# Deferring the second LayerNorm of the later half of the tokens into the first down projection

## Chip, cores, metric

One core of one Trainium2 chip for each run; the experiments ran in three groups, each on its own chip with its own runs of the kernel before. The metric is the device time of one execution in microseconds (us), median of several runs. The engines are called PE (matrix multiply), DVE (vector), ACT (scalar activation), Pool (GpSimd) and SP (whose queue issues all DMAs of this kernel).

## The reference

A linear attention block and a gated MLP, each behind a LayerNorm, with residuals; S = 2048 tokens, D = 1024, F = 3584, bf16.

```python
h  = x + attention(layernorm(x)) @ wo            # 32 heads, phi(t) = elu-like feature map
n  = layernorm(h)
h2 = h + (relu(n @ W_gate) * (n @ W_up)) @ W_down
```

## The kernel before

The tokens are 16 tiles of 128. The attention half of the kernel walks over tile steps `t`. At step `t` PE computes the numerators of tile `t` (`a2`, eight short matmuls), DVE divides (`dtmp`, `rden`, three products), a DMA transposes the result, and two steps later (`LAG = 2`) PE applies the output projection (`a4`, 16 matmuls of 512 columns) and DVE adds the residual. In steps 0 to 10 two query projections (`a1`, 8 matmuls each, with an exp on ACT and two DVE operations behind them) fill PE. Then the MLP runs in two passes of 1024 tokens: first 14 gate/up pairs by a Strassen scheme that needs sums of activations (S sums) and of weights (T sums), then four down rounds of 24 us.

```python
        def a4(st):
            ...                                  # 16 matmuls into a pair of banks
            PL.add("dve", ... name="h_%d" % st)  # hsb = psum + x2  (residual)
            dma(sl_hs[hs], h_scr[st * P:(st + 1) * P, :], hsb[:, hs, :], "st_h_%d" % st, ...)
            ks = ln_stats(hsb[:, hs, :], ...)    # DVE: 2 bn_stats, aggregate, +eps; Pool: rstd (pow)
            PL.add("pool", ... name="nmr_%d" % st)          # -mean * rstd
            ...
        def a4_norm(st):                         # one step later
            PL.add("act", ... name="norm2_%d" % st)         # ACT: xn = rstd * h + nmr
            if st < TPP:                         # first 8 tiles: straight to the MLP's input
                dma_t(sl_tx[kx], hnT[:, :, st * P:(st + 1) * P], xn[:, kx, :], "T5d_%d" % st, ...)
            else:                                # later 8 tiles: scratch copy for the second pass
                dma(sl_tx[kx], hn_scr[(st - TPP) * P:(st - TPP + 1) * P, :], xn[:, kx, :], ...)
        ...                                      # (cut)
        for t in range(NST + LAG + 1):
            if t >= LAG + 1:
                a4_norm(t - LAG - 1)
            if t < NST:
                a2(t)
            if rest:
                a1(*rest.pop(0))
            if LAG <= t < NST + LAG:
                a4(t - LAG)
            if rest:
                a1(*rest.pop(0))
            if t == 13:
                s_sums()                         # DVE, 4 x 1.2 us
            if t == 15:
                for f_ in t_sums(0) + t_sums(1): # DVE, 8 x 0.42 us
                    f_()
        ...                                      # (cut) d_round: seven steps of 16 matmuls
            for c in range(NFB):
                ...                              # 16 matmuls; in the last step also the evictions
                load_wd_next()                   # next weight tile, 4 steps ahead
                if fill:
                    fill.pop(0)()                # extra work handed in, one piece a step
```

In the traces the instructions of an engine start in the order in which the program lists them.

## Time and profile before

| | |
|---|---|
| median time | 801.71 us (801.42 to 802.7, 3 runs) |
| PE busy | 777.7 of the profiled 800.3 us (97%) |
| DVE / ACT / Pool busy | 54% / 31% / 3% |
| chain that ended last | 91% PE, 5% DVE |

PE is full nearly everywhere; the exception is the seam between attention and MLP. The table of windows of the kernel before shows it (columns: window and length, then busy us and instruction count of PE, PE weight loads, DVE, ACT and Pool, then the granted PE clock, DMA share and GB/s):

```profile
core 0: us, PE busy (x) PEld busy (x) DVE busy (x) ACT busy (x) POOL busy (x), PEclk, DMA share, GB/s
200.00:225.00 25.00, 24.66 (x135) 11.93 (x134) 23.05 (x52) 8.20 (x10) 3.07 (x8) 1.00 0.56 142
225.00:250.00 25.00, 17.35 (x83) 7.55 (x84) 23.23 (x47) 3.72 (x3) 4.65 (x8) 0.87 0.68 157
250.00:275.00 25.00, 20.08 (x84) 8.57 (x84) 17.24 (x37) 9.88 (x13) 2.74 (x7) 0.93 0.53 179
```

PE loses 7.6 us in the second and 4.9 us in the third window, and the clock is below 1.00 there, while DVE is nearly full in the first two. The PE timeline of the kernel before shows where (columns: start, length, engine, line, operation, count; in brackets the idle time before it and what ended it):

```profile
start us, us, engine line op out<-in xcount [idle before <-releaser]
...
220.22 0.63 PE L499 MATMUL ps<-kvz,RAB 128*128 128x132 bf16 x8
...
235.99 3.61 PE L499 MATMUL ps<-RW,RO 128*128 128x512 bf16 x15
245.15 1.45 PE L499 MATMUL ps<-kvz,RAB 128*128 128x132 bf16 x8 [5.55 <-DVE RO L674]
246.39 12.43 PE L499 MATMUL ps<-RW,RO 128*128 128x512 bf16 x47
258.66 1.89 PE L499 MATMUL ps<-hnT,wring 128*128 128x512 bf16 x8
260.39 1.89 PE L499 MATMUL ps<-RC,RE 128*128 128x512 f16 x8
267.10 3.42 PE L499 MATMUL ps<-RC,RE 128*128 128x512 f16 x8 [4.82 <-ACT ps L762]
270.31 1.89 PE L499 MATMUL ps<-hnT,wring 128*128 128x512 bf16 x7
```

At warm pace 16 matmuls of 512 columns take 3.45 us to the start of the next group. So 5.55 us are lost before 245.15, 4.82 us before 267.10, and matmuls after each of these gaps are slow (eight took 3.21 us to the next group's start instead of 1.73). The first gap has its cause in DVE, as the DVE timeline of the kernel before shows: the S sums (L735) stand ahead of the division (L663) of the tile that PE wants next:

```profile
238.87 2.36 DVE L735 TENSOR_TENSOR RC<-hnT 128x2048 f16<-128x2048 bf16 x2
241.26 1.22 DVE L735 TENSOR_TENSOR RC<-RC,hnT 128x2048 f16<-128x2048 f16 x1
242.52 1.23 DVE L735 TENSOR_TENSOR RC<-hnT,RC 128x2048 f16<-128x2048 bf16 x1
243.67 0.38 DVE L663 TENSOR_SCALAR dtmp<-ps 128x24 f32<-128x24 f32 x2
```

The second gap is a chain: residual, statistics of the last tile, rstd, norm2 on ACT, and only then ACT's first copy for the MLP, which PE waits for. Its end, in the ACT timeline of the kernel before (L717 is norm2, L762 the copies):

```profile
265.32 1.24 ACT L717 ACTIVATE xn<-hsb,nmr,rstd 128x1024 bf16<-128x1024 bf16 x1 [1.91 <-POOL nmr L706]
266.46 1.06 ACT L762 ACTIVATE ps<-ps 128x512 f32<-128x512 f32 x2
```

As one yardstick for the seam, take the time from `a2` of tile 11 (220.22) to the MLP's second product on the plain weights (270.31): 50.09 us. At warm pace it is 5 x 0.47 (`a2`) + 7 x 3.45 (`a4`) + 3 x 1.73 (the first three MLP products) = 31.7 us. The seam loses 18.4 us, 2.3% of the kernel.

### The profile page before, as it was taken

The numbers are of one execution on the slowest core, as the hardware profiler recorded it, in microseconds if no ns is written. First come the engines' busy times: TensorE is split into PE (matmuls) and PEld (weight loads), VectorE is DVE, ScalarE is ACT, GpSimd is POOL, SyncE is SP. The second block draws the span as 40 slices with busy tenths as digits, with TensorE's granted clock in tenths as the row PEclk, the third lists the DMA queues.
The fourth block names the chain that finished last, engine by engine and source line by source line (L and its number), as shares of the span: only waits on it lengthen the run. The fifth ranks groups of instructions, "written<-read, shape, count | busy, mean of one in ns | idle before, by whom it ended". The sixth has DMA issues, their size and how long they took to land.

```text
span 800.3 us, 9969 instructions
## 1 busy us (share of the span) xinstructions
PE 777.7 (97%) x3719; PEld 360.3 (45%) x3791; DVE 432.3 (54%) x900; ACT 246.8 (31%) x402; POOL 25.2 (3%) x60
## 2 busy tenths in 40 slices
PE   8999999999987799999999999999999999999998
PEld 3444444444433344444444444444444444444443
DVE  7455535799999656756755103137657657401111
ACT  4333333232321455455453000024454454400000
POOL 2000000010111000000000000000000000000000
PEclk9999999999998999999999999999999999999999
DMA  9777300155574523223234896643133132035662
GB/s 302 197 182 199 94 14 1 34 139 140 140 174 127 188 74 105 77 83 106 69 89 131 230 243 211 206 135 106 54 105 104 55 106 80 0 125 192 209 207 82
DMA packets 160128, 102.37 MB, mean 128 GB/s; under 512 B 50384, under 2 KB 153040, under 8 KB 160080
## 3 DMA queue, kind: packets, MB, share of 16 engines
q1 hardware_dynamic: 160080, 101.73, 43.9%
q8 instruction: 30, 0.49, 0.3%
q14 instruction: 18, 0.15, 0.1%
HBM read 79.69 MB, written 10.49 MB: 113 GB/s over the span
## 4 chain that ended last, share of the span: by engine, by line
PE 91%; DVE 5%; issue 1%; DMA 1%; ACT 1%; SPq 0%; POOL 0%; DVEq 0%; POOLq 0%; ACTq 0%
PE ps L499 91%; DVE st L509 1%; DVE hsb L698 1%; DVE RO L674 1%; DMA RAB<-in_A_wqkv_dram 1%; ACT RX L533 1%; DVE RAB L538 1%; DVE RC L735 0%; DVE RX L535 0%; DVE RE L751 0%; DVE rden L667 0%; DVE dtmp L663 0%; SPq L432 0%; DVE mv L512 0%; PE ps L568 0%
## 5 line engine op out<-in xcount | busy, mean ns | idle before, releaser
L499 PE MATMUL ps<-RW,RAB 128*128 128x512 bf16 x878 | 192.8, 379 | 0.9
L499 PE MATMUL ps<-RC,RE 128*128 128x512 f16 x672 | 155.9, 382 | 4.8 <-ACT ps L762 4.8
L499 PEld LDWEIGHTS ps<-RW,RAB 128*128 128x128 bf16 x896 | 87.7, 98 | 105.7
L499 PE MATMUL ps<-RAB 128*128 128x512 bf16 x499 | 112.4, 379 | 1.7 <-ACT RAB L571 0.7
L762 ACT ACTIVATE ps<-ps 128x512 f32<-128x512 f32 x112 | 65.1, 582 | 152.9 <-PE ps L499 149.1
L868 DVE TENSOR_TENSOR RX<-ps,RX 128x512 bf16<-128x512 f32 x32 | 22.0, 691 | 166.1 <-PE ps L499 145.3
L499 PE MATMUL ps<-hnT,wring 128*128 128x512 bf16 x448 | 106.0, 379 | 0.0
L499 PEld LDWEIGHTS ps<-RC,RE 128*128 128x128 f16 x672 | 66.0, 98 | 85.2 <-ACT ps L762 5.3
L762 ACT ACTIVATE RO<-ps 128x512 f32<-128x512 f32 x112 | 66.7, 597 | 53.7 <-PE ps L499 53.7
L812 DVE TENSOR_TENSOR RAB<-ps,RAB 128x512 bf16<-128x512 f32 x28 | 19.4, 691 | 112.8 <-PE ps L499 112.8
L499 PEld LDWEIGHTS ps<-RAB 128*128 128x128 bf16 x512 | 49.2, 98 | 58.0 <-ACT RAB L571 0.9
L499 PEld LDWEIGHTS ps<-hnT,wring 128*128 128x128 bf16 x448 | 43.9, 98 | 53.3 <-issue 0.8
L533 ACT ACTIVATE RX<-ps 128x512 bf16<-128x512 f32 x64 | 38.0, 594 | 92.5 <-PE ps L499 65.8
L499 PE MATMUL ps<-RW,RO 128*128 128x512 bf16 x249 | 59.1, 388 | 0.4
L499 PE MATMUL ps<-RAB,RC 128*128 128x512 bf16 x250 | 58.0, 379 | 0.3
L499 PE MATMUL ps<-RC,wring 128*128 128x512 f16 x224 | 52.9, 379 | 0.0
L762 ACT ACTIVATE RAB<-ps 128x512 bf16<-128x512 f32 x56 | 33.4, 597 | 62.2 <-PE ps L499 62.2
L535 DVE TENSOR_SCALAR RX<-RX 128x512 bf16<-128x512 bf16 x64 | 18.4, 288 | 58.6 <-ACT RX L533 58.6
L499 PE MATMUL ps<-hnT,RE 128*128 128x512 bf16 x196 | 46.9, 379 | 1.5
L751 DVE TENSOR_TENSOR RE<-wring,RE 128x512 f16<-128x512 bf16 x112 | 47.0, 420 | 1.9
L751 DVE TENSOR_TENSOR RE<-wring 128x512 f16<-128x512 bf16 x112 | 42.0, 416 | 0.0
L819 DVE TENSOR_TENSOR RO<-ps,RO 128x512 f32<-128x512 f32 x56 | 38.7, 691 | 5.5 <-ACT RO L762 5.4
(56 smaller groups left out, 486.3 us busy)
## 6 DMA issues: line engine op xcount, KB each, us to landing
RW<-in_B_W_down_dram SPq DMA_DIRECT2D x56, 512.0 KB, 3.7
wring<-in_B_W_gate_dram SPq DMA_DIRECT2D x28, 512.0 KB, 3.7
wring<-in_B_W_up_dram SPq DMA_DIRECT2D x28, 512.0 KB, 4.7
RAB<-in_A_wqkv_dram SPq DMA_DIRECT2D x8, 512.0 KB, 8.4
RX<-in_A_x_dram SPq DMA_DIRECT2D x16, 256.0 KB, 3.1
h_scr<-hsb SPq DMA_DIRECT2D x16, 256.0 KB, 3.3
RX<-h_scr SPq DMA_DIRECT2D x32, 128.0 KB, 3.7
out_dram<-RX SPq DMA_DIRECT2D x32, 128.0 KB, 1.7
```

Source lines behind the costliest of these rows:

```text
L499: lambda e: e.matmul(out_ap, lhsT, rhs, start=start, stop=stop, skip_group_check=skip),
L509: PL.add("dve", lambda e, c=c: e.bn_stats(out=st6[:, k, c * 6:(c + 1) * 6], in_=src_full[:, c * BCH:(c + 1) * BCH]), reads=[src_chunk_bufs ...
L533: PL.add("act", lambda e: e.activation(out=Et[:, k, 0:w], in_=src, func=ACTF.Exp), reads=[B_bank[b]], writes=[B_E[k]], name=name + "_exp")
L535: PL.add("dve", lambda e: e.tensor_scalar(out=E2t[:, k, 0:w], in0=Et[:, k, 0:w], scalar1=1.0, scalar2=1e-6, op0=ALU.min, op1=ALU.add), rea ...
L538: PL.add("dve", lambda e: e.scalar_tensor_tensor(out=dst_ap, in0=src, scalar=C1, in1=E2t[:, k, 0:w], op0=ALU.add, op1=ALU.max), reads=[B_b ...
L674: lambda e, nbk=nbk, g0=g0, ng=ng: e.tensor_tensor(out=osb[:, k, g0 * P:(g0 + ng) * P].rearrange("p (g h e) -> p g h e", g=ng, e=Dh), in0= ...
L698: PL.add("dve", lambda e: e.tensor_tensor(out=hsb[:, hs, :], in0=ps[:, b:b + 2, :], in1=x2[:, xs, :].rearrange("p (a c) -> p a c", a=2), o ...
L751: PL.add("dve", lambda e: e.tensor_tensor(out=Tring[:, k, j], in0=in0, in1=in1, op=ALU.subtract), reads=reads, writes=[B_T[k][j]], name="T ...
L762: PL.add("act", lambda e: e.activation(out=dst, in_=src, func=func), reads=reads, writes=writes, name=name)
L812: PL.add("dve", lambda e: e.tensor_tensor(out=hh[:, f1, 0:SBW], in0=bank(BA[1]), in1=r11[:, rr, :], op=ALU.mult), reads=[B_bank[BA[1]], B_ ...
L819: PL.add("dve", lambda e, w=w: e.tensor_tensor(out=ftmp[:, 4 + w, :], in0=bank(BF_[w]), in1=ftmp[:, 2 + w, :], op=ALU.add), reads=[B_bank[ ...
L868: PL.add("dve", lambda e: e.tensor_tensor(out=outst[:, k, :], in0=bank(banks4[j], NW), in1=hres[:, k, :], op=ALU.add), reads=[B_bank[banks ...
```

## The change

The LayerNorm of tiles 8 to 15 is needed only in the second MLP pass. The change takes it out of the seam, where DVE is short, and puts it into the first two down rounds, where DVE is nearly idle (before the change 2.77 us busy in 450 to 475): each of ten down steps loads one tile of `h` back, computes statistics on the tile before it, and normalizes (on DVE) and transposes the tile before that. The scratch copy of the normalized tiles goes away. The first eight T sums go to Pool at step 8, and the S sums come one step earlier.

```diff
+            if st >= TPP:
+                return                          # in a4: no statistics for tiles 8..15
             ks = ln_stats(hsb[:, hs, :], [B_hs[hs]] * NBC, "ln2_%d" % st)
...
-            else:
-                dma(sl_tx[kx], hn_scr[...], xn[:, kx, :], "st_hn_%d" % st, ...)
+        def late_ln(i):
+            def load(t):
+                dma(sl_hl[t % 2], hl[:, t % 2, :], h_scr[(TPP + t) * P:(TPP + t + 1) * P, :], ...)
+            def stats(t):
+                late_k[t] = ln_stats(hl[:, t % 2, :], [B_hl[t % 2]] * NBC, ...)
+            def norm(t):
+                ln_norm_dve(late_k[t], hl[:, k, :], [B_hl[k]], xl[:, k, :], B_xl[k], ...)
+                dma_t(sl_xl[k], hnT[:, :, t * P:(t + 1) * P], xl[:, k, :], "T5d_%d" % (TPP + t), ...)
+            if 0 <= i - 2 < TPP:
+                norm(i - 2)
+            if i < TPP:
+                load(i)
+            if 0 <= i - 1 < TPP:
+                stats(i - 1)
...
-            if t == 13:
+            if t == 8:
+                for f_ in t_sums(0, "pool") + t_sums(1, "pool"):
+                    f_()
+            if t == 12:
                 s_sums()
-            if t == 15:
-                for f_ in t_sums(0) + t_sums(1):
-                    f_()
...
-                    for t in range(i * STB, (i + 1) * STB):
-                        late.append(... dma_t(..., hn_scr[t * P:(t + 1) * P, :], "T5s_%d" % t, ...))
+                    for t in range(i * NFB, (i + 1) * NFB):
+                        late.append(lambda t=t: late_ln(t))
```

(`hl` and `xl` lie in memory that the attention half no longer uses.)

More of the change, by code (lines that the diff above doesn't have):

```diff
@@ L191, in bass_sequential_preLN__linear_attn_block__glu_gated_reglu__prompt_kernel @@
     h_scr = nc.dram_tensor("h_scr", [S, D], bf16).ap()
-    hn_scr = nc.dram_tensor("hn_scr", [S // 2, D], bf16).ap()
     es = ExitStack()
@@ L243, in bass_sequential_preLN__linear_attn_block__glu_gated_reglu__prompt_kernel @@
         Tring = RE[:, 0:NTR * 4 * KH * P].bitcast(f16).rearrange("p (s j k c) -> p s j k c", s=NTR, j=4, k=KH)
+        o0 = NTR * 4 * KH * P
+        hl = RE[:, o0:o0 + 2 * D].rearrange("p (a b) -> p a b", a=2)
+        xl = RE[:, o0 + 2 * D:o0 + 4 * D].rearrange("p (a b) -> p a b", a=2)
         RO = sb("RO", [P, 2 * NO * D], bf16)
@@ L305, in bass_sequential_preLN__linear_attn_block__glu_gated_reglu__prompt_kernel @@
         sl_hs = slots("dhs_", NHS)
-        sl_ht = slots("dht_", TPP)
+        sl_hl = slots("dhl_", 2)
+        sl_xl = slots("dxl_", 2)
         def bufs(name, n):
@@ L331, in bass_sequential_preLN__linear_attn_block__glu_gated_reglu__prompt_kernel @@
         B_hscr = bufs("hscr_", NST)
-        B_hnscr = bufs("hnscr_", TPP)
+        B_hl = bufs("hl_", 2)
+        B_xl = bufs("xl_", 2)
         B_st6 = [bufs("st6_%d_" % k, NBC) for k in range(NSTAT)]
@@ L362, in flat @@
             return [b for row in x for b in (flat(row) if isinstance(row, list) else [row])]
-        for b_ in flat(B_T):
+        for b_ in flat(B_T) + B_hl + B_xl:
             b_.over = flat(B_x1) + flat(B_pk) + flat(B_v)
@@ L421, in bass_sequential_preLN__linear_attn_block__glu_gated_reglu__prompt_kernel @@
         PL.add("pool", lambda e: e.memset(vv[:, :, :, P:VW], 1.0), writes=[B_vones], name="vones")
-        for b_ in flat(B_T):
+        for b_ in flat(B_T) + B_hl + B_xl:
             b_.over = b_.over + [B_vones]
@@ L719, in a4_norm @@
                    reads=[B_hs[hs], B_nmr[ks], B_rstd[ks]], writes=[B_xn[kx]], name="norm2_%d" % st)
-            if st < TPP:
-                dma_t(sl_tx[kx], hnT[:, :, st * P:(st + 1) * P], xn[:, kx, :], "T5d_%d" % st, reads=[B_xn[kx]],
-                      writes=[B_hnT[st]])
-            else:
-                dma(sl_tx[kx], hn_scr[(st - TPP) * P:(st - TPP + 1) * P, :], xn[:, kx, :], "st_hn_%d" % st,
-                    reads=[B_xn[kx]], writes=[B_hnscr[st - TPP]])
+            dma_t(sl_tx[kx], hnT[:, :, st * P:(st + 1) * P], xn[:, kx, :], "T5d_%d" % st, reads=[B_xn[kx]],
+                  writes=[B_hnT[st]])
+        late_k = {}
+        def late_ln(i):
+            def load(t):
+                dma(sl_hl[t % 2], hl[:, t % 2, :], h_scr[(TPP + t) * P:(TPP + t + 1) * P, :], "ld_hl_%d" % t,
+                    reads=[B_hscr[TPP + t]], writes=[B_hl[t % 2]])
+            def stats(t):
+                late_k[t] = ln_stats(hl[:, t % 2, :], [B_hl[t % 2]] * NBC, "ln2_%d" % (TPP + t))
+            def norm(t):
+                k = t % 2
+                ln_norm_dve(late_k[t], hl[:, k, :], [B_hl[k]], xl[:, k, :], B_xl[k], "ln2_%d" % (TPP + t))
+                dma_t(sl_xl[k], hnT[:, :, t * P:(t + 1) * P], xl[:, k, :], "T5d_%d" % (TPP + t), reads=[B_xl[k]],
+                      writes=[B_hnT[t]])
+            if 0 <= i - 2 < TPP:
[4 more added lines that the diff above has]
+                stats(i - 1)
         def s_sums():
@@ L741, in s_sums, with t_sums @@
             add(3, blk(1, 0), Ssum[:, 1], ALU.subtract, [B_S[1]] + bl(0))
-        def t_sums(L):
+        def t_sums(L, eng="dve"):
             i = L % NWG
@@ L750, in add @@
             def add(j, in0, in1, reads):
-                PL.add("dve", lambda e: e.tensor_tensor(out=Tring[:, k, j], in0=in0, in1=in1, op=ALU.subtract),
+                PL.add(eng, lambda e: e.tensor_tensor(out=Tring[:, k, j], in0=in0, in1=in1, op=ALU.subtract),
                        reads=reads, writes=[B_T[k][j]], name="T%d_%d" % (j + 1, L))
@@ L964, in bass_sequential_preLN__linear_attn_block__glu_gated_reglu__prompt_kernel @@
         for t in range(NST + LAG + 1):
-            if t >= LAG + 1:
+            if LAG + 1 <= t < TPP + LAG + 1:
                 a4_norm(t - LAG - 1)
@@ L994, in bass_sequential_preLN__linear_attn_block__glu_gated_reglu__prompt_kernel @@
                 if p_ + 1 < NPASS and i < 2:
-                    for t in range(i * STB, (i + 1) * STB):
-                        late.append(lambda t=t: dma_t(
-                            sl_ht[t], hnT[:, :, t * P:(t + 1) * P], hn_scr[t * P:(t + 1) * P, :],
-                            "T5s_%d" % t, reads=[B_hnscr[t]], writes=[B_hnT[t]]))
+                    for t in range(i * NFB, (i + 1) * NFB):
+                        late.append(lambda t=t: late_ln(t))
                 if p_ + 1 < NPASS and i == 2:
```

## The prediction

> **What bounds the kernel now.** TensorE. The page has PE busy for 777.7 of 800.3 us (97%), and the chain that ended last is 91% PE. It is full (24.9 of every 25 us, clock 1.00) everywhere except in the first microseconds and at the seam between attention and MLP: the table of 25 us windows shows 17.35 us busy at 225-250 (clock 0.87) and 20.08 at 250-275 (clock 0.93). There DVE is busy for 23.2 and 17.2 us. The PE timeline at the seam shows idle stretches of 0.8 us at three tiles, 5.55 us at 239.6 (DVE does the four S sums, 4.9 us, ahead of a tile's division) and 4.82 us at 262.3 (PE waits for ACT's first copy, which stands behind norm2 of the last tile, hence behind that tile's statistics). About 5 us more go to matmuls that run slower after the gaps (47 in 12.4 us; warm pace 16 in 3.45). Against an ideal pace the seam loses some 17-18 us. That is all this change can win.
>
> **Removed.** For 8 tiles: two bn_stats of 0.69, aggregate 0.21, add 0.15 = 1.7 us of DVE each, 14 us in all; rstd 0.55 + nmr 0.27 on Pool; norm2 1.24 on ACT; one 256 KB store. Eight T sums (0.42 us each, 3.4 us) leave DVE. Once the a1 projections run out (tile step 11 on) a step needs 5.3 us of DVE against 4.05 us of PE; without LayerNorm DVE needs 3.7, so PE becomes the limit. The 4.82 us wait at the end disappears.
>
> **Kept.** The S sums still sit before a tile's division, one step earlier: about 4-5 us of PE wait, 1-2 us of it again in slow matmuls.
>
> **New cost 1, Pool.** Eight tensor_tensor of 512 elements per partition. No such Pool op is in this trace. The Trainium skill, "GPSIMD Engine Reference", section 3.1, gives 4497 ns for 2048 elements; my estimate from it is 1.1-1.3 us each, 9-11 us together, starting at about 208 us. rstd of tile 7 queues behind them (218-219 us instead of 214.6), norm2 of tile 7 on ACT is late, the exp behind it too, then DVE, then the bank pair for the next output projection: I charge 2-3 us of PE wait near 221. The skill's "SBUF — State Buffer" (section Who interferes with whom) says that DVE and Pool lock a shared port pair; the trace agrees so far: rstd took 1.60 us instead of 0.55 beside the S sums. A few e2 ops (0.29 us) on DVE may wait about 1 us each.
>
> **New cost 2, the first down rounds.** 8 x (1.7 + 0.54 norm) = 18 us of DVE where DVE is nearly idle (2.8 of 25 us), 2 MB more reads. DMA is already at 0.9-1.2 there while transposes run, but weight tiles are issued four steps (about 10 us) ahead; I expect PE to stay full: 0-1 us.
>
> **Sum.** 17.5 - 5.5 (S sums with slow clock) - 2.5 (Pool) + about 1.5 (other) = about 11 us saved: 790.7 us, range 786.5 to 795.5. Faster by over 2%: 0.09; within 2%: 0.89; slower: 0.02.
>
> **What would show it.** The first MLP matmul at about 247-250 us instead of 258.7, with no wait for ACT after it; one remaining gap of 3.5-5 us around 232-236, released by DVE; Pool T sums above 1 us each and a PE gap of 2-3 us near 221; PE full from 425 to 535 us.
>
> **What would make it wrong.** Pool sums at 2 us or more each (S sums then wait for tile 7's transpose, several us back); or at 0.6 us (2-3 us more gain); DMA saturation in the first down rounds starving the weights; the clock staying low after the gap.

## The result

| | before | changed |
|---|---|---|
| median time | 802.08 us (801.42 to 802.7, 4 runs) | 792.8 us (792.4 to 793.36, 4 runs) |
| ratio | 1 | 0.9885 (95%: 0.9868 to 0.9902) |
| profiled span | 800.3 us | 790.9 us |
| seam (50.09 us before) | loses 18.4 us | loses 7.7 us |

A ratio is the mean time of one kernel's runs over that of the other's of the same rounds, so it is not quite the ratio of the medians. The change is 1.15% faster: clear of the noise, and within 2%.

The windows of the changed kernel (the last line is in the down rounds):

```profile
core 0: us, PE busy (x) PEld busy (x) DVE busy (x) ACT busy (x) POOL busy (x), PEclk, DMA share, GB/s
...
225.00:250.00 25.00, 20.79 (x108) 9.54 (x109) 20.26 (x36) 0.00 (x0) 0.00 (x0) 0.93 0.68 155
250.00:275.00 25.00, 25.00 (x117) 11.35 (x116) 13.74 (x27) 10.44 (x18) 0.00 (x0) 1.00 0.50 158
...
450.00:475.00 25.00, 23.85 (x112) 10.51 (x110) 12.73 (x26) 0.00 (x0) 2.19 (x4) 1.00 0.94 252
```

DVE is no longer full at the seam and PE gained 3.4 and 4.9 us there; the third window is full. A small new loss stands at 450-475. The PE timeline of the changed kernel at the seam:

```profile
220.29 0.63 PE L504 MATMUL ps<-kvz,RAB 128*128 128x132 bf16 x8
...
225.08 0.35 PE L504 MATMUL ps<-kvz,RAB 128*128 128x132 bf16 x3 [0.71 <-DVE RO L679]
...
226.26 3.62 PE L504 MATMUL ps<-RW,RO 128*128 128x512 bf16 x16
...
230.79 3.63 PE L504 MATMUL ps<-RW,RO 128*128 128x512 bf16 x16 [0.45 <-DMA RO<-RO]
237.38 0.35 PE L504 MATMUL ps<-kvz,RAB 128*128 128x132 bf16 x3 [2.96 <-DVE RO L679]
...
238.56 5.30 PE L504 MATMUL ps<-RW,RO 128*128 128x512 bf16 x16
243.70 0.63 PE L504 MATMUL ps<-kvz,RAB 128*128 128x132 bf16 x8
...
254.53 1.89 PE L504 MATMUL ps<-hnT,wring 128*128 128x512 bf16 x8
...
259.71 1.89 PE L504 MATMUL ps<-hnT,wring 128*128 128x512 bf16 x8
```

From 220.29 to 259.71 are 39.42 us, 7.7 us over the 31.7 us of warm pace. Three things make it up:

- From the end of the projection before it (about 224.2 at warm pace) to 226.26, 2.04 us pass for an `a2` of 0.47 us: 1.57 us lost. At 230.79 another 0.6 us, where a transpose came late.
- At 234.24 (230.79 + 3.45) PE stops until 237.38 for the division of tile 13, behind the S sums; `a4` starts at 238.56 instead of 234.71: 3.85 us.
- The 16 matmuls after it take 243.70 - 238.56 = 5.14 us instead of 3.45: 1.69 us of low clock.

The sum is 7.71 us. The wait for ACT before the MLP is gone. The Pool timeline of the changed kernel shows the first item's origin, the sums (L777, two in a line) between rstd of tile 6 and rstd of tile 7 (L522):

```profile
207.27 0.55 POOL L522 TENSOR_TENSOR rstd<-ve,neghalf 128x1 f32<-128x1 f32 x1 [6.46 <-DVE ve L519]
...
208.50 2.27 POOL L777 TENSOR_TENSOR RE<-wring 128x512 f16<-128x512 bf16 x2 [0.32 <-issue]
...
215.33 2.43 POOL L777 TENSOR_TENSOR RE<-wring,RE 128x512 f16<-128x512 bf16 x2
217.72 0.55 POOL L522 TENSOR_TENSOR rstd<-ve,neghalf 128x1 f32<-128x1 f32 x1
```

One Pool sum took 1.13 to 1.22 us, and rstd of tile 7, at 214.57 before, came at 217.72.

The loss in the down rounds is one gap of PE, 1.15 us, and what ended it was a weight load:

```profile
423.74 38.15 PE L504 MATMUL ps<-RW,RAB 128*128 128x512 bf16 x176
463.04 58.94 PE L504 MATMUL ps<-RW,RAB 128*128 128x512 bf16 x272 [1.15 <-DMA RW<-in_B_W_down_dram]
```

The DMA issues of the changed kernel around it (RW is the weight ring; columns as in the timeline, length is the issue's time in the queue):

```profile
447.84 1.48 SPq L441 DMA_TRANSPOSE hnT<-RE  x1
...
450.81 2.12 SPq L437 DMA_DIRECT2D out_dram<-RX  x4
453.03 0.39 SPq L437 DMA_DIRECT2D RW<-in_B_W_down_dram  x1
...
455.43 1.92 SPq L437 DMA_DIRECT2D RX<-h_scr  x4
457.44 0.38 SPq L437 DMA_DIRECT2D RW<-in_B_W_down_dram  x1
```

A step of the round takes 3.45 us, so with the round beginning at 423.74 PE ends its seventh step at about 447.9 and its eighth at 451.3 (estimates by that count; in the first step the load went out 0.3 us after the time so counted, at 427.45). The weight loads that these ends allow were issued at 453.03 and 457.44, 5 and 6 us late; the second landed 5.55 us after its issue, by the chain of waits, at 462.99, and PE went on at 463.04. What stood ahead of it in the queue: a transpose of a deferred tile (1.2 to 1.5 us of queue time each; its own wait is for norm on DVE), four output stores that waited for evictions (on DVE these began at 450.09, behind the statistics of a deferred tile, which had waited for its load until 448.45), and four residual loads (1.92 us).

The two ends meet: the seam gained 18.4 - 7.7 = 10.7 us, the down rounds lost 1.2 us, so 9.5 us should be gained; the spans differ by 9.4 us.

### The profile page after: what moved, and what is told of

The parts are those of the page before. It is cut to its first block, busy times and chain, and to the rows that moved or that the text cites. A ratio compares the mean times of both kernels' runs of the same rounds, so it can differ in the third digit from the quotient of the medians.

```text
span 790.9 us, 10017 instructions
## 1 busy us (share of the span) xinstructions
PE 779.6 (99%) x3791; PEld 360.0 (46%) x3791; DVE 434.4 (55%) x900; ACT 237.3 (30%) x394; POOL 30.5 (4%) x60
## 4 chain that ended last, share of the span: by engine, by line
PE 95%; DVE 2%; issue 1%; DMA 1%; SPq 1%; ACT 0%; POOL 0%; DVEq 0%; POOLq 0%
PE ps L504 95%; DMA RW<-in_B_W_down_dram 1%; DVE RO L679 1%; DVE RC L761 0%; SPq L437 0%; DVE RX L894 0%; PE ps L573 0%; DVE hsb L703 0%; SPq L441 0%; DVE rden L672 0%; DVE dtmp L668 0%; DVE RX L540 0%; ACT RX L538 0%; DVE RAB L543 0%; POOL hsb L399 0%
## 5 line engine op out<-in xcount | busy, mean ns | idle before, releaser
L504 PE MATMUL ps<-RC,RE 128*128 128x512 f16 x672 | 154.2, 380 | 0.0
L540 DVE TENSOR_SCALAR RX<-RX 128x512 bf16<-128x512 bf16 x64 | 19.5, 305 | 61.3 <-ACT RX L538 61.2
L504 PE MATMUL ps<-hnT,RE 128*128 128x512 bf16 x224 | 52.9, 380 | 0.0
L777 DVE TENSOR_TENSOR RE<-wring,RE 128x512 f16<-128x512 bf16 x108 | 45.5, 421 | 1.8
L777 DVE TENSOR_TENSOR RE<-wring 128x512 f16<-128x512 bf16 x108 | 40.6, 418 | 0.0
```

What stands on the lines that cost most here:

```text
L504: lambda e: e.matmul(out_ap, lhsT, rhs, start=start, stop=stop, skip_group_check=skip),
L540: PL.add("dve", lambda e: e.tensor_scalar(out=E2t[:, k, 0:w], in0=Et[:, k, 0:w], scalar1=1.0, scalar2=1e-6, op0=ALU.min, op1=ALU.add), rea ...
L777: PL.add(eng, lambda e: e.tensor_tensor(out=Tring[:, k, j], in0=in0, in1=in1, op=ALU.subtract), reads=reads, writes=[B_T[k][j]], name="T%d ...
```

## The experiments

The theory after reading the traces: (1) the deferral alone makes the gain; (2) the Pool sums cost, because rstd of tile 7 stands behind them in Pool's queue; (3) the S sums' place, not their work, makes the 5.5 us that remain; (4) the down rounds' gap comes from the order in SP's queue. Rivals: DVE and Pool contend for their shared port (against 2); the S sums' time cannot be hidden (against 3); the DMA engines are simply saturated (against 4). Eleven kernels ran; all results were correct.

### Pool sums one step later

```diff
-            if t == 8:
+            if t == 9:
                 for f_ in t_sums(0, "pool") + t_sums(1, "pool"):
```

> The eight weight sums on Pool are issued one tile step later (step 9), behind tile 7's rstd and nmr. Theory (queue): the PE gap near 224-226 (1.6 us over pace) and the late transpose wait at 230 (0.6 us) came from rstd of tile 7 standing behind 9.4 us of sums in Pool's queue, then norm2 on ACT, the exp behind it, DVE. So rstd of tile 7 returns to about 214.6, the gap near 224 goes, 1.5 to 2.2 us saved: about 790.9. Rival (shared port): DVE's e2 ops waited for Pool's sums (0.56 and 1.02 us instead of 0.28), which the move keeps, so the gap stays and the time stays within 0.4 us of the changed kernel's 792.8.

Measured: 791.42 us, ratio to before 0.986. rstd of tile 7 was back at 214.26, and the wait near 224 fell from 1.57 to 0.14 us; the seam lost 6.3 us. The gain of about 1.4 us over the changed kernel is just below the expected 1.5 to 2.2; in the profiled run the down rounds' gap, which this edit does not touch, was 1.82 us instead of 1.15. The run does not refute the shared port alone, because DVE's e2 operations (a short one behind each exp, L540 of the changed kernel), which took 0.56 and 1.02 us instead of 0.28 beside the Pool sums of the changed kernel, happened not to meet them here (0.28 to 0.33 us). The dose test below separates the two.

### The Pool sums done twice

```diff
             if t == 8:
-                for f_ in t_sums(0, "pool") + t_sums(1, "pool"):
+                for f_ in t_sums(0, "pool") + t_sums(1, "pool") + t_sums(0, "pool") + t_sums(1, "pool"):
```

> The changed kernel with the eight Pool sums done twice (same values): dose test of the queue. rstd of tile 7 then waits 9.4 us longer, to about 227. Theory (queue): norm2 of tile 7 at about 228 holds the last two exps, DVE and PE; the gap near 224 grows from about 1.6 to 10 us or more (and slow matmuls follow), 803 to 806. If only the shared port mattered, some more e2 ops would wait up to 1 us each and the time would rise by less than 2 us.

Measured: 802.68 us, ratio 1.0003: all that the change gained was lost again, by Pool work whose results were already there. In the Pool timeline of this run rstd of tile 7 came 8.8 us later than in the changed kernel, and the PE timeline shows one gap of 8.16 us half way through an output projection, ended by the DVE operation behind the late exp (L543):

```profile
226.48 0.55 POOL L522 TENSOR_TENSOR rstd<-ve,neghalf 128x1 f32<-128x1 f32 x1
```

```profile
230.44 3.27 PE L504 MATMUL ps<-RW,RO 128*128 128x512 bf16 x8 [8.16 <-DVE RAB L543]
```

The seam lost 48.37 - 31.7 = 16.7 us, 9.0 more than in the changed kernel, for 8.8 us more of queue. The e2 operations beside the sums took the same 0.55 and 1.02 us as in the changed kernel. So the queue is the cause, and the port's share is small. My expected range was a little too high: 8 us of gap, not 10 or more, and 802.68 us, not 803 to 806. Of the 10.5 us between this profiled span and that of the changed kernel (801.4 and 790.9), 9.0 lie in the seam; the down rounds, which the edit does not touch, had gaps of 0.94 and 2.03 us instead of one of 1.15.

### First T sums back on DVE

```diff
-            if t == 8:
-                for f_ in t_sums(0, "pool") + t_sums(1, "pool"):
-                    f_()
             if t == 12:
                 s_sums()
+            if t == 15:
+                for f_ in t_sums(0) + t_sums(1):
+                    f_()
```

> The changed kernel with the first weight sums back on DVE at step 15 (S sums stay at step 12): undoes the Pool part alone. Theory: with the LayerNorm gone DVE has room at step 15, so the 3.4 us cost nothing there, and the gap near 224 goes with the Pool sums: 1.5 to 2.2 us faster than the changed kernel, about 791. Rival (the change's own idea, that the sums have to leave DVE): a new PE wait of up to 3 us before the MLP, 794 to 796.

Measured: 791.16 us, ratio 0.9859: 1.6 us faster than the changed kernel, and the seam lost 6.2 us, against 6.3 with the sums at step 9. With the LayerNorm gone, DVE has room for the T sums at step 15. The Pool part of the change cost 1.6 us and brought nothing.

### The Pool part without the deferral

The edit is to the kernel before; its LayerNorm stays where it was.

```diff
-            if t == 13:
+            if t == 8:
+                for f_ in t_sums(0, "pool") + t_sums(1, "pool"):
+                    f_()
+            if t == 12:
                 s_sums()
-            if t == 15:
-                for f_ in t_sums(0) + t_sums(1):
-                    f_()
```

> The kernel before with the weight sums on Pool at step 8 and the S sums at step 12, but without the deferred LayerNorm: the Pool part alone. Theory: the deferral is what made PE the limit after step 10; without it the Pool part takes about 2 us off the last wait (4.82 us before the MLP's first T product) and adds about 1 to 2 us near 224: 800 to 802.5, within 0.3% of before. Rival (relieving DVE of 3.4 us of sums is worth about that): 798.5 or less.

Measured: 803.63 us (801.64 to 803.85), ratio 1.0018 (1.0004 to 1.0032): 1.4 us slower than before, 1.1 us beyond the expected range. The last wait fell from 4.82 to 2.77 us, as expected, but near 226 a gap of 2.54 us arose, and the 16 matmuls behind it took 6.00 us to the next group instead of 3.45:

```profile
226.56 1.45 PE L499 MATMUL ps<-kvz,RAB 128*128 128x132 bf16 x8 [2.54 <-DVE RO L674]
227.80 6.16 PE L499 MATMUL ps<-RW,RO 128*128 128x512 bf16 x16
233.80 0.63 PE L499 MATMUL ps<-kvz,RAB 128*128 128x132 bf16 x8
...
268.42 1.90 PE L499 MATMUL ps<-RC,RE 128*128 128x512 f16 x8 [2.77 <-ACT ps L762]
```

The profiled execution is the fastest of the five (801.64 us); the other four took 803.5 us or more. So the gain of the change comes from the deferral. The S sums' move by one step, from 13 to 12, was never run alone; it is part of this run, which gained nothing with it.

### S sums behind the last division

```diff
-            if t == 8:
+            if t == 9:
                 for f_ in t_sums(0, "pool") + t_sums(1, "pool"):
...
-            if t == 12:
+            if t == 15:
                 s_sums()
```

> As the run with the weight sums at step 9, and the S sums on DVE moved from step 12 to step 15, behind the last division and tile 13's residual add. Theory: the gap at 234-237.4 and the slow matmuls after it (together about 5.5 us) exist only because 4.9 us of S sums stand ahead of tile 13's division; at step 15 PE has two output projections (6.9 us) that need nothing from them, so gap and slow clock go: 5 to 6 us less than the run with step 9 alone, about 785.5. Rival: the 4.9 us of DVE only move; PE then waits for tile 14's or 15's bank or for the S sums before the second MLP product, and less than 2 us are gained.

Measured: 785.09 us (784.41 to 786.45), ratio 0.9789 (0.9775 to 0.9802): 6.3 us less than with step 9 alone. The profiled spans differ by 6.9 us: 5.6 us are the seam (6.3 us lost there, now 0.7); nearly all of the rest lies in the down rounds, untouched by this edit, whose gap was 1.82 us in the one profiled run and 0.36 us in the other. The PE timeline of this run shows no gap at the place of the old one, nor slow matmuls behind it:

```profile
232.46 0.63 PE L504 MATMUL ps<-kvz,RAB 128*128 128x132 bf16 x8
232.93 3.61 PE L504 MATMUL ps<-RW,RO 128*128 128x512 bf16 x16
236.38 0.63 PE L504 MATMUL ps<-kvz,RAB 128*128 128x132 bf16 x8
236.85 10.52 PE L504 MATMUL ps<-RW,RO 128*128 128x512 bf16 x48
247.21 1.89 PE L504 MATMUL ps<-hnT,wring 128*128 128x512 bf16 x8
```

The same 4.9 us of DVE work cost about 5.5 us of PE ahead of tile 13's division and nothing behind tile 13's residual, because there PE has two projections and the MLP's first product (8.6 us) that need nothing of it.

### The down rounds: another order in the queue

```diff
...                                              # (cut: d_store and load_hr hold the DMAs taken from their old places)
                 load_wd_next()
+                if c == NFB - 1:
+                    for j in range(STB):
+                        d_store(j)              # output stores behind the weight load
                 if fill:
                     fill.pop(0)()
+                if c == 2:
+                    load_hr()                   # residual loads here, not at the round's start
```

> The changed kernel with another order in SP's DMA queue in the down rounds: the next weight tile is issued ahead of a round's four output stores, and the four residual loads are issued after the third step of the round instead of at its start. Bytes and DVE work are the same. Theory (queue order): the 1.15 us PE gap at 462-463 came from a weight load issued 5.9 us late (457.4 instead of 451.5), because SP waits in order for evictions that stand behind statistics on DVE, and then issues four loads (1.9 us) first; with the new order that load goes out 2 us or more earlier and the gap goes: about 791.6. Rival (DMA saturation): the load's 5.55 us of flight at a DMA share of 1.1 to 1.36 is the cause; the order does not change the bytes, and a gap of about 1 us stays.

Measured: 793.04 us, ratio 0.9887: no gain. The gap at 462 went, but a new one of 2.08 us stood at 471.9, at the start of the third round:

```profile
473.97 48.51 PE L504 MATMUL ps<-RW,RAB 128*128 128x512 bf16 x224 [2.08 <-DVE RC L761]
```

The profile names DVE's S sums as what ended it, but PE does not read them there; what it needs is a weight tile. Its load had been allowed at about 461.3 (by the same step count) and was issued at 469.6, behind a transpose that waited for the deferred chain and behind the residual loads, which were now in the middle of the second round. So my cure was wrong. The gap moved with the order at equal bytes, which speaks for the queue; that this load ended the second gap is inferred, not shown.

### The down rounds: a pause at the round's end

```diff
-                    for t in range(i * NFB, (i + 1) * NFB):
-                        late.append(lambda t=t: late_ln(t))
+                    for t in ([0, 1, 2, 3, 4, None, None] if i == 0 else [5, 6, 7, 8, 9]):
+                        late.append((lambda: None) if t is None else (lambda t=t: late_ln(t)))
```

> The changed kernel with the deferred LayerNorm's steps paused at the last two steps of the first down round (five steps, pause of two, five steps). Theory (queue order): no statistics wait for a load ahead of the evictions, so the evictions start when PE ends each tile (about 445.6 instead of 450.1), no weight load is over 3 us late, the gap of 1.15 us goes: about 791.6. Rival (DMA saturation): the same 10 steps with the same bytes still follow each other, only the pause relieves; the gap moves into the second round or stays.

Measured: 791.16 us, ratio 0.9864, where the run with the other order, on the same chip, had 0.9887. All 448 matmuls of the four rounds ran without a gap:

```profile
423.79 96.86 PE L504 MATMUL ps<-RW,RAB 128*128 128x512 bf16 x448
```

The DMA share was 0.95 and 0.97 in 425-450 and 450-475, against 1.03 and 0.94 in the changed kernel: about as busy as before. But the first round's evictions began at 446.06 instead of 450.09, and the weight loads behind the round's end, at 453.03 and 457.44 in the changed kernel, went out at 449.82 and 452.32, by the same step count about 1.9 and 0.9 us late instead of 5 and 6:

```profile
446.79 2.93 SPq L437 DMA_DIRECT2D out_dram<-RX  x4
449.82 0.41 SPq L437 DMA_DIRECT2D RW<-in_B_W_down_dram  x1
...
452.32 0.38 SPq L437 DMA_DIRECT2D RW<-in_B_W_down_dram  x1
```

Why the changed kernel falls behind is a reading of its issues, which no run tested apart (the pause changes the order on DVE and in SP's queue together): eight transposes of deferred tiles between 435.70 and 467.98 make 4.6 us a tile (32.28 / 7), longer than PE's step of 3.45 us. A tile's load, statistics, rstd, norm and transpose form a loop through two buffers, and the weight loads sit in the same queue. By this reading the pause lets the queue catch up before the evictions. That the flight of 5.55 us under a busy DMA had a part in the 1.15 us is likely (the median over the kernel is 3.7), but alone it made no gap: in the run with the pause weight loads issued between 440 and 470 took up to 5.5 us to land.

### The down rounds: every second step

```diff
-                if p_ + 1 < NPASS and i < 2:
-                    for t in range(i * NFB, (i + 1) * NFB):
-                        late.append(lambda t=t: late_ln(t))
-                if p_ + 1 < NPASS and i == 2:
+                if p_ + 1 < NPASS and i < 3:
+                    for c in range(i * NFB, (i + 1) * NFB):
+                        late.append((lambda t=c // 2: late_ln(t)) if c % 2 == 0 else (lambda: None))
+                if p_ + 1 < NPASS and i == 3:
                     late.append(s_sums)
```

> The changed kernel with a deferred LayerNorm step at every second down step instead of every one (over three rounds, S sums of the second half at the fourth round). Both theories expect the 1.15 us gap to go (about 791.6); the DMA share in 425-475 us should fall from 0.95-1.03 to about 0.8. If S sums at the last round come too late, a PE wait at the start of the second MLP half (522 us) of some us would show; I expect none, since the round has 24 us.

Measured: 791.4 us, ratio 0.9867, and again no gap in the rounds. The DMA share did not fall as I expected: 0.78, then 1.02, and 0.91 at 475-500. So here too a window at full DMA share starved nothing.

The gap in the down rounds varies from run to run, so one profile proves little. But in all five profiled runs that kept the changed kernel's order there, PE lost 0.36 to 2.97 us to weight loads, and in all five with the pause or with every second step (these two and the three below) it lost nothing.

### All three moves together

Against the changed kernel:

```diff
-            if t == 8:
+            if t == 9:                           # T sums on Pool
...
-            if t == 12:
+            if t == 15:                          # S sums
...
-                    for t in range(i * NFB, (i + 1) * NFB):
+                    for t in ([0, 1, 2, 3, 4, None, None] if i == 0 else [5, 6, 7, 8, 9]):   # the pause
```

> Three moves together: Pool's weight sums at step 9, S sums at step 15, the deferred LayerNorm paused at the end of the first down round. The gaps lie in different stages, so the gains should add: 785.1 less about 1.5 us, that is 783.3 to 784, with PE showing no gap over 0.5 us after the first 25 us. If the gap at 462 had been only a shift of idle time, nothing would be gained over 785.1.

Measured: 783.71 us (783.31 to 784.5), ratio 0.9769 (0.9755 to 0.9782), 2.3% faster than before. PE had one wait of 0.59 us, for a transpose, where I expected none over 0.5. Part of the gain is not settled: in the profiled run of the version without the pause the down rounds' gap was only 0.36 us, against 1.15 and 1.82 us in others, and the two profiled spans are equal (782.7 and 782.8); the medians differ by 1.4 us, on different chips.

The same with the deferred LayerNorm at every second step (the edit shown above) in place of the pause:

> As the run with the pause, but with the deferred LayerNorm at every second down step. Same PE-bound time expected, 783.3 to 784.3, within 0.5 us of the run with the pause.

Measured: 783.98 us, ratio 0.9771. No difference.

The version with the pause, without the Pool part:

```diff
-            if t == 9:
-                for f_ in t_sums(0, "pool") + t_sums(1, "pool"):
-                    f_()
             if t == 15:
                 s_sums()
+                for f_ in t_sums(0) + t_sums(1):
+                    f_()
```

> As the run with the pause, but without the Pool part: the first weight sums run on DVE behind the S sums at step 15. DVE then has 8.3 us between tile 13's and tile 14's residual adds, against 6.9 us of output projections and 1.7 us of the first MLP products on PE. If the Pool part has any worth in the best order, this run shows a PE wait of 0.5 to 3 us before the second or third MLP product (784 to 787); if not, it equals the run with the pause within 0.5 us.

Measured: 784.2 us, ratio 0.9776. PE had one wait of 0.48 us, for ACT's copy, where the version with Pool had the one of 0.59 us. Both the wait and the time, 0.5 us above the run with the pause, lie on the border between my two expectations. In the best order too the Pool part is worth nothing that these runs resolve.

## Why the prediction was right, and where it was not

- **The limit and the stake.** Right: everything that could be won lay at the seam. I put it at 17 to 18 us; by the yardstick it was 18.4.
- **The S sums stay and cost 5.5 us.** Right: 3.85 us of wait and 1.69 us of slow matmuls. I placed the gap at 232-236; PE stood from 234.2 to 237.4.
- **Pool.** Right in mechanism and size: 1.13 to 1.22 us a sum (estimate 1.1 to 1.3), rstd of tile 7 at 217.7 (218 to 219 estimated), 1.57 + 0.6 us lost (2 to 3 estimated), at 224 rather than 221. Only the last link differs: PE waited for the division of the next tile (L679), which stood on DVE behind the late exps' operations, and not for the bank pair of a projection; in the run with the sums done twice PE stopped for the operation that frees a bank of a projection (L543). The estimate came from the Trainium skill, "GPSIMD Engine Reference", section 3.1: 4497 ns for 2048 fp32 elements, a quarter of which is 1.12 us; the trace agrees, though the sums here are not fp32. The skill's "SBUF — State Buffer", section Who interferes with whom, says that the port pair that DVE and Pool share is locked by one of them at a time; this fits two e2 operations of 0.28 us that took 0.56 and 1.02 us beside the sums.
- **Down rounds.** The term was 0 to 1 us, and it measured 1.15. I argued that weights issued 10 us ahead are safe, and looked only at DMA bandwidth; the trace shows the 10 us used up by 6 us of late issue and 5.55 us of flight. This overlap is what the prediction had wrong.
- **The sum.** The named terms for the seam give 17.5 - 5.5 - 2.5 = 9.5 us. The seam gained 10.7: 0.9 us more because the stake was 18.4, and 0.3 us more because Pool cost 2.17. I had added "about 1.5 (other)" without naming a cause, so it was luck that it came near these 1.2 us. The down rounds' loss was left out of the sum: 10.7 less 1.2 is 9.5, and the medians give 9.3. The forecast of 11 was 1.7 us too high, and 792.8 lies inside the range.
- **A wrong sign to look for.** I wrote that the first MLP matmul would come at 247 to 250 us. That contradicted my own sum: such a time leaves no room for the two losses that I had just charged. It came at 254.53, and at 247.21 in the run where both losses had been removed.

## What to carry to other kernels

Taking work off a busy engine pays where that engine holds up the limiting one; then see what still stands in program order ahead of the result that the limiting engine wants next. Here moving 4.9 us of S sums by three steps was worth 5.6 us, while moving 3.4 us of T sums to an idle engine cost 1.6 us, because a 0.55 us operation that ACT, DVE and PE needed stood behind them. And a prefetch distance is time only while the queue that issues the prefetch is not made to wait for a slower chain.

## What the Trainium skill lacked or had wrong

- "GPSIMD Engine Reference", section 3.1, gives its tensor_tensor figure for fp32 only. With bf16 inputs and fp16 output, 512 elements per partition took 1.13 to 1.22 us on Pool here, about a quarter of its 4497 ns. If time goes with the number of elements, which no run tested, the narrower type brought nothing.
- "TensorE: Matmul & The Clock Gate", section Why this matters for your kernels, advises against idle gaps over about 3 us. Here shorter ones could be enough: after 2.54 us 16 matmuls took 6.00 us instead of 3.45, after 2.96 us 5.14 us. But length alone did not decide: after 2.77 us in the same run as the 2.54, eight matmuls took their 1.73 us, and after 2.08 us (the other order in the down rounds) 16 took 3.45 us. What else decides, these runs do not show.
- "DMA: Bandwidth & Descriptors" gives the queue time of a transpose only in a table of cycles that compares the next chip with previous generations, and for other cases than this kernel's: small tiles from HBM (631 cycles in previous generations) and 8,192 tiles within SBUF. Here, within SBUF, the transpose of one 128 x 1024 tile took 1.24 us and more of SP's queue, over three times the 0.38 us of a plain load of 512 KB. One such transpose stands with its 1.24 us in the chain ahead of the weight load that PE waited for at 463.
